# A gated recurrent cell and a tanh-shrink dense layer: the activation as a short polynomial, with a test and a second pass behind it

## The chip, the cores and the metric

One core of a Trainium2 chip. The metric is the device time of one execution of the whole kernel, in microseconds; lower is better.

## What is computed

The first half is an mLSTM cell over 4 x 8 heads, 768 steps and 40 features per head; the kernel computes it in chunks of 128 steps. Its output, rearranged to 3072 tokens of 320 features, goes through a dense pair of products with an activation between them:

```
def _moe_ref(x, w_in, w_out):
    h = x @ w_in            # 3072 x 320 by 320 x 2048
    g = h - np.tanh(h)
    return (g @ w_out).astype(np.float32)   # 2048 x 320
```

`w_in` and `w_out` arrive as 64-bit floats and are turned into 32-bit floats on the chip. All products are 32-bit.

## The kernel before

**The cell.** A unit is one chunk of one batch entry: 6 chunks x 4 entries make 24 units `n`. `cell_slot` (before L433) writes one slot of the cell: it fetches the inputs of the next unit (`fetch`), makes the decay matrix `E` of unit `s` by a scan on VectorE (`decay`, L348), takes its scores on TensorE (`score`, with the multiply by `E` on VectorE in L380), and for an older unit `o` the output (`inter`, `intra`), its normalisation (`gate`, L402 to L407) and the new state (`update`: product `pc`, then two adds on VectorE in L420). For a third unit `x` it transposes the result (`turn`, `px`, L89) and copies it into `xT` on ScalarE (L431). `ph`, `pc` and `px` share the two buffers of one PSUM pool, so `px` can only be written when the adds in L420 have emptied `pc`.

**The weights.** `convert` takes each 64-bit block apart: `w_e` and `w_m` on VectorE (L280, L283), then three ScalarE instructions (L281, L284, L285), then two on GpSimd (`w_r`, L286 and L287), then the sign on VectorE (L291), which writes `w_in` or `w_out`. There are 40 such blocks.

**The dense part.** Two units make a group `g` of 256 tokens, 12 groups; the 2048 hidden columns are 8 pairs `p` of 256. An item is one group by one pair, 96 in all. For an item `up` makes `h` in PSUM (`ph_up`, 6 products, each recorded as two instructions), `shrink` makes `g` in `gt`, and two items later (`LAG`) `down` adds 4 products into `po` (also two instructions each). `shrink` in the kernel before is four ScalarE instructions (L488 to L491: square, tanh, the square of a shifted square, and a mask) and five VectorE instructions (L492 to L496): a polynomial in `gt`, `h - tanh(h)` in `t`, and a copy of `t` into `gt` where `h` squared is over 0.1225:

```
A.activation(out=t, in_=ph, func=AF.Tanh)
A.activation(out=big, in_=z, func=AF.Relu, bias=border)
V.tensor_tensor(out=t, in0=ph, in1=t, op=OP.subtract)
V.copy_predicated(gt, big.bitcast(I32), t)
```

**The order.** Groups 0 to 5 are done in three passes over parts of the pairs (`PASSES`: pairs 0 and 1, 2 to 4, 5 to 7), since the weights of the later pairs are not converted yet. The first pass (12 items) is written between the cell's slots, about one item to a slot; the second pass (18 items) between the conversions of the last blocks; the remaining cell slots are spread over the later items. TensorE's order is fixed by hand (class `T` chains each of its instructions to the last). The other engines' orders come from the scheduler, and each engine runs its own in order. Loads are issued on SyncE's queue, the stores of the output on ScalarE's. All DMAs of both queues take eight completion semaphores in turn, and a DMA waits for the one that had its semaphore before.

Of the kernel before, what the change touches and what calls it, by code (L numbers as in the profile page):

```python
# [28 lines left out]
FP = mybir.dt.float32  # L32
BF = mybir.dt.bfloat16
I32 = mybir.dt.int32
I64 = mybir.dt.int64
U32 = mybir.dt.uint32
AF = mybir.ActivationFunctionType
OP = mybir.AluOpType
PSUM = bass.MemoryType.PSUM
NO_SYNC = mybir.DependencyInfo(mybir.DependencyClass.NoSync, mybir.DependencyReason.DATA)  # L40

L = 128


POLY = (-0.019838061344260048, -2.6070109206805303, -0.05287600604508702, 6.442407825412434)
# [9 lines left out]
def kernel(  # L55
# [13 lines left out]
    nc = tc.nc  # L69
    V, A, G = nc.vector, nc.scalar, nc.gpsimd  # L70
# [20 lines left out]
    B, NT, D, H, _ = qT.shape  # L91
    D1 = D + 1
    BH, S = i_gate.shape
    DM, DFF = moe_w_in.shape
    NFF = DFF // 128
    KC = [(c, min(128, DM - c)) for c in range(0, DM, 128)]
    NK = len(KC)
    NU = B * NT
    GT = 2
    TG = GT * L  # L100
    NG = NU // GT
    NP = NFF // 2
    HH = H // 2
    LAG = 2
    FIRST = 6
    NX = FIRST + 1
    PASSES = ((0, 1), (2, 4), (5, NP - 1))

    const = ctx.enter_context(tc.tile_pool(name="const", bufs=1))
    load = ctx.enter_context(tc.tile_pool(name="load", bufs=2))  # L110
    dram = ctx.enter_context(tc.tile_pool(name="dram", bufs=1, space=bass.MemoryType.DRAM))
    att = ctx.enter_context(tc.tile_pool(name="att", bufs=2))
    conv = ctx.enter_context(tc.tile_pool(name="conv", bufs=2))
    mlp = ctx.enter_context(tc.tile_pool(name="mlp", bufs=2))
    ps_h = ctx.enter_context(tc.tile_pool(name="ps_h", bufs=2, space=PSUM))
    ps_o = ctx.enter_context(tc.tile_pool(name="ps_o", bufs=1, space=PSUM))
    ps_a = ctx.enter_context(tc.tile_pool(name="ps_a", bufs=2, space=PSUM))
# [12 lines left out]
    TOP = SEC + D  # L130
    kz = [const.tile([128, H, L], FP, name=f"kz{i}") for i in range(2)]
    q2 = [const.tile([128, HH, L], FP, name=f"q2{i}") for i in range(2)]
    kp = [const.tile([L, HH, TOP], FP, name=f"kp{i}") for i in range(4)]
    v1 = [const.tile([L, H, D1], FP, name=f"v1{i}") for i in range(3)]
    for i in range(4):
# [9 lines left out]
    def load_unit(n):  # L145
# [7 lines left out]
        for r0, h0 in ((0, 0), (SEC, HH)):  # L153
            nc.sync.dma_start(out=t["kp"][:, :, r0:r0 + D], in_=k[b, c, :, h0:h0 + HH])
        t["o"] = load.tile([L, H, D], FP, name="o", tag="o", bufs=4)
        nc.sync.dma_start(out=t["o"], in_=o_gate[b, c])
# [6 lines left out]
    ones = const.tile([128, TOP], FP, name="ones")  # L163
    diag = const.tile([128, H, L], BF, name="diag")
    rebias = const.tile([128, 1], FP, name="rebias")
    square = const.tile([128, 1], FP, name="square")
    border = const.tile([128, 1], FP, name="border")
    V.memset(rebias, -896.0 * (1 << 23))
    V.memset(square, POLY[2])
    V.memset(border, -SMALL)  # L170
    make_identity(nc, ident)
    V.memset(ones, 1.0)
# [30 lines left out]
    for w in (after, ones):  # L203
        p = ps_b.tile([w.shape[1], NT, BH], FP, name="psum_lf", tag="b")
        T.matmul(p.rearrange("p c n -> p (c n)"), w, lfT.rearrange("p c n -> p (c n)"),
                 start=True, stop=True)
# [10 lines left out]
    xr, n, f = (mlp.tile([L, 2, NR], FP, name=name, tag=tag) for name, tag in (("xr", "z"), ("n", "z"), ("f", "q")))  # L217
# [34 lines left out]
    w_in = const.tile([128, NK, DFF], FP, name="w_in")  # L252
    w_out = const.tile([128, NFF, DM], FP, name="w_out")
# [63 lines left out]
    xT = [const.tile([128, NK, TG], FP, name=f"xT{i}") for i in range(NX)]  # L317
# [5 lines left out]
    for t in xT + qg + ys + sum(state, []):  # L323
        G.memset(t, 0.0)


    un = {}

# [95 lines left out]
    def turn(n, j):  # L424
        t = un[n]
        if j == 0:
            t["px"] = ps_b.tile([128, NK, L], FP, name="px", tag="b")
        T.transpose(t["px"][:, j, :], t["y"][:, j * 128:(j + 1) * 128], ident)
        if j == NK - 1:
            g, tt = divmod(n, GT)  # L430
            A.copy(out=xT[g % NX][:, :, tt * L:(tt + 1) * L], in_=t["px"])  # L431
            un.pop(n)

    def cell_slot(s, o, x):


        steps = []

        def begin():
            if o is not None:  # L440
                prepare(o)
            if s is not None and s - 1 in un:
                prepare(s - 1)
            if s is not None:
                if s + 1 < NU:
                    fetch(s + 1)
                decay(s)

        steps.append((0.0, begin))
        for d in range(HH):  # L450
            for i in range(2):
                if s is not None:
                    steps.append((0.22, lambda h=2 * d + i: score(s, h)))
                if o is not None and i == 0:
                    steps.append((0.22 if o >= B else 0.0, lambda d=d: inter(o, d)))
            if o is not None:
                steps += [(0.22, lambda h=h: intra(o, h)) for h in (d, d + HH)]
                if d in (1, 2) and o + B < NU:
                    steps += [(0.18, lambda j=j: update(o, j)) for j in (2 * d - 2, 2 * d - 1)]
        if o is not None:  # L460
            steps.append((0.0, lambda: gate(o)))
        if x is not None:
            steps += [(0.11, lambda j=j: turn(x, j)) for j in range(NK)]
        return steps


    gT, po = {}, {}
    lead, root, _, rest = POLY

    def up(g, p):  # L470
        ph = {}

        def product(i, j):
            if not ph:
                ph[0] = ps_h.tile([128, 2, TG], FP, name="ph_up", tag="ph")
            f = 2 * p + i
            T.matmul(ph[0][:, i, :], w_in[:, j, f * 128:(f + 1) * 128], xT[g % NX][:, j, :],
                     start=(j == 0), stop=(j == NK - 1))
            if (i, j) == (1, NK - 1):
                shrink(ph[0])  # L480

        def shrink(ph):
            z = mlp.tile([128, 2, TG], FP, name="z", tag="z")
            q = mlp.tile([128, 2, TG], FP, name="q", tag="q")
            t = mlp.tile([128, 2, TG], FP, name="t", tag="t")
            big = mlp.tile([128, 2, TG], FP, name="big", tag="big")
            gt = gT[g, p] = mlp.tile([128, 2, TG], FP, name="gt", tag="gt", bufs=LAG + 2)
            A.activation(out=z, in_=ph, func=AF.Square)  # L488
            A.activation(out=t, in_=ph, func=AF.Tanh)  # L489
            A.activation(out=q, in_=z, func=AF.Square, bias=square)  # L490
            A.activation(out=big, in_=z, func=AF.Relu, bias=border)  # L491
            V.scalar_tensor_tensor(out=gt, in0=ph, scalar=lead, in1=z, op0=OP.mult, op1=OP.mult)  # L492
            V.tensor_tensor(out=t, in0=ph, in1=t, op=OP.subtract)  # L493
            V.scalar_tensor_tensor(out=gt, in0=z, scalar=root, in1=gt, op0=OP.add, op1=OP.mult)  # L494
            V.scalar_tensor_tensor(out=gt, in0=q, scalar=rest, in1=gt, op0=OP.add, op1=OP.mult)  # L495
            V.copy_predicated(gt, big.bitcast(I32), t)  # L496

        return [(0.43, lambda i=i, j=j: product(i, j)) for i in range(2) for j in range(NK)]

# [96 lines left out]
        merge(dense, work[x])  # L596


# [39 lines left out]
```

## Time and profile before

| | |
|---|---|
| runs, median of 3 | 707.3 us (707.11 to 708.67) |
| profiled execution | 708.27 us, of it the span of instructions 706.6 us |
| TensorE matmuls | busy 625.3 us (89%) |
| VectorE | busy 541.0 us (77%) |
| ScalarE | busy 303.4 us (43%) |
| GpSimd | busy 164.5 us (23%) |
| TensorE's mean granted clock | 0.934 of full speed |
| DMA | 50.93 MB |

The shares are means over a span with two halves. Up to about 300 us the cell, the conversions and 21 items share the engines; after that 75 items and the rest of the cell run. So the table by stretches is what is to be read, then what each engine waits for in a stretch.

### The profile page before, as it was taken

What the parts mean: (1) busy time and instruction counts of PE and PEld (TensorE: products, weight loads), DVE (VectorE), ACT (ScalarE), POOL (GpSimd) and SP (SyncE); (2) the same over time, 40 slices, a digit from 0 to 9 for tenths busy, and PEclk for the clock granted to TensorE, in tenths of its full rate; (3) what the DMA queues carried; (4) which work ended last, traced back from release to release, by engine and by line L of the source; (5) the groups of instructions that cost most, each with busy time, mean ns of one, the idle gap of its engine ahead of it and who ended that gap; (6) DMA issues with size and microseconds to landing.
All of it is one profiled execution on the core that took longest, in us unless ns stands there. A gap on an engine that the chain in (4) does not pass through costs nothing.

```text
span 706.6 us, 9050 instructions
## 1 busy us (share of the span) xinstructions
PE 625.3 (89%) x3098; PEld 520.4 (74%) x3098; DVE 541.0 (77%) x897; ACT 303.4 (43%) x584; POOL 164.5 (23%) x190
## 2 busy tenths in 40 slices
PE   1277797797888985999999999999999999999997
PEld 1276696685777863678888888888888888878875
DVE  8677778887888798987768797776866766767764
ACT  3323143343532476654444343444534435454553
POOL 7535544445443267400002011010110000000000
PEclk9757689998988997999999999999999999999999
DMA  5657345554464443100003132220200000000000
GB/s 141 161 150 205 103 118 139 150 158 108 125 170 115 141 126 78 37 1 2 0 24 100 30 95 57 71 72 6 91 10 0 20 1 19 1 20 0 10 10 20
DMA packets 73278, 50.93 MB, mean 72 GB/s; under 512 B 53520, under 2 KB 60048, under 8 KB 73232
## 3 DMA queue, kind: packets, MB, share of 16 engines
q1 hardware_dynamic: 69360, 46.22, 23.8%
q10 hardware_dynamic: 3872, 4.13, 1.7%
q8 instruction: 25, 0.41, 0.2%
q14 instruction: 21, 0.17, 0.1%
HBM read 46.20 MB, written 4.13 MB: 71 GB/s over the span
## 4 chain that ended last, share of the span: by engine, by line
PE 69%; DVE 16%; POOL 5%; ACT 4%; issue 4%; DMA 2%; SPq 1%; ACTq 0%; POOLq 0%; DVEq 0%
PE ph_up L85 31%; PE po L85 25%; PE ps L85 5%; PE ph L85 5%; DVE E L348 3%; POOL w_r L286 2%; POOL w_r L287 2%; PE pc L85 1%; DVE gt L495 1%; DVE gt L494 1%; DVE gt L492 1%; DVE t L493 1%; DVE w_in L291 1%; PE px L89 1%; DVE E L380 1%
## 5 line engine op out<-in xcount | busy, mean ns | idle before, releaser
L85 PE MATMUL ph_up<-xT,w_in 128*128 128x256 f32 x1152 | 307.8, 394 | 2.3 <-DVE t L493 1.6
L85 PE MATMUL po<-w_out,gt 128*128 128x320 f32 x768 | 249.1, 449 | 10.7 <-DVE part L514 9.8
L85 PEld LDWEIGHTS ph_up<-xT,w_in 128*128 128x128 f32 x1152 | 209.7, 196 | 36.7 <-issue 3.9
L85 PEld LDWEIGHTS po<-w_out,gt 128*128 128x128 f32 x768 | 138.8, 195 | 49.7 <-DVE part L514 12.1
L488 ACT ACTIVATE z<-ph_up 128x512 f32<-128x512 f32 x96 | 57.2, 596 | 269.1 <-PE ph_up L85 263.5
L492 DVE SCALAR_TENSOR_TENSOR gt<-ph_up,z 128x512 f32<-128x512 f32 x96 | 66.0, 687 | 90.8 <-ACT t L489 90.7
L85 PE MATMUL ps<-q,kz 128*128 128x128 f32 x384 | 85.0, 323 | 17.5 <-DVE E L380 11.7
L85 PEld LDWEIGHTS ps<-q,kz 128*128 128x128 f32 x384 | 74.3, 228 | 25.8 <-DVE E L380 11.9
L496 DVE COPY_PREDICATED gt<-big,t 128x512 f32<-128x512 int32 x96 | 76.5, 796 | 6.5 <-DVE gt L495 0.5
L85 PEld LDWEIGHTS ph<-vw,E 128*128 128x128 f32 x384 | 69.4, 214 | 7.9
L495 DVE SCALAR_TENSOR_TENSOR gt<-q,gt 128x512 f32<-128x512 f32 x96 | 70.1, 730 | 6.5 <-DVE gt L494 0.5
L490 ACT ACTIVATE q<-z,square 128x512 f32<-128x512 f32 x96 | 69.4, 723 | 0.0
L491 ACT ACTIVATE big<-z,border 128x512 f32<-128x512 f32 x96 | 69.1, 720 | 0.0
L494 DVE SCALAR_TENSOR_TENSOR gt<-z,gt 128x512 f32<-128x512 f32 x96 | 67.5, 703 | 0.0
L493 DVE TENSOR_TENSOR t<-ph_up,t 128x512 f32<-128x512 f32 x96 | 65.3, 680 | 0.0
L85 PE MATMUL ph<-vw,E 128*128 128x41 f32 x384 | 61.9, 267 | 0.0
L489 ACT ACTIVATE t<-ph_up 128x512 f32<-128x512 f32 x96 | 56.8, 592 | 0.0
L348 DVE TENSOR_TENSOR_SCAN E<-E,diag 128x1024 f32<-128x1024 f32 x24 | 55.8, 2324 | 0.8 <-DMA E<-f_rows 0.8
L363 POOL TENSOR_TENSOR qg<-qg,q 104x512 f32<-104x512 f32 x20 | 28.2, 1410 | 117.4 <-DMA qg<-g_rows 90.1
L286 POOL TENSOR_TENSOR w_r<-w_r,w_m 128x256 f32<-128x256 f32 (+2 forms) x40 | 36.3, 907 | 56.2 <-ACT w_m L284 43.1
L366 POOL TENSOR_TENSOR vs<-v,eiS 128x328 f32<-128x328 f32 x20 | 17.7, 884 | 108.8 <-PE pc L85 108.8
L89 PE MATMUL px<-ident,ys 128*128 128x128 f32 x72 | 17.0, 305 | 26.5 <-DVE state L420 23.5
(87 smaller groups left out, 489.4 us busy)
## 6 DMA issues: line engine op xcount, KB each, us to landing
E<-f_rows SPq DMA_DIRECT2D x24, 512.0 KB
w<-in_moe_w_out SPq DMA_DIRECT2D x16, 320.0 KB
w<-in_moe_w_in SPq DMA_DIRECT2D x16, 256.0 KB
kz<-in_kT SPq DMA_DIRECT2D x48, 80.0 KB
q<-in_qT SPq DMA_DIRECT2D x48, 80.0 KB
v<-in_v SPq DMA_DIRECT2D x24, 160.0 KB
kp<-in_k SPq DMA_DIRECT2D x48, 80.0 KB
o<-in_o_gate SPq DMA_DIRECT2D x24, 160.0 KB
```

The lines of the kernel that those rows point to most:

```text
L85: return cls.keep(nc.tensor.matmul(*args, **kwargs))
L286: G.tensor_tensor(out=rf, in0=rf, in1=mf, op=OP.add)
L348: V.tensor_tensor_scan(out=row, data0=row, data1=diag.rearrange("p h t -> p (h t)"), initial=0.0, op0=OP.mult, op1=OP.add)
L488: A.activation(out=z, in_=ph, func=AF.Square)
L489: A.activation(out=t, in_=ph, func=AF.Tanh)
L490: A.activation(out=q, in_=z, func=AF.Square, bias=square)
L491: A.activation(out=big, in_=z, func=AF.Relu, bias=border)
L492: V.scalar_tensor_tensor(out=gt, in0=ph, scalar=lead, in1=z, op0=OP.mult, op1=OP.mult)
L493: V.tensor_tensor(out=t, in0=ph, in1=t, op=OP.subtract)
L494: V.scalar_tensor_tensor(out=gt, in0=z, scalar=root, in1=gt, op0=OP.add, op1=OP.mult)
L495: V.scalar_tensor_tensor(out=gt, in0=q, scalar=rest, in1=gt, op0=OP.add, op1=OP.mult)
L496: V.copy_predicated(gt, big.bitcast(I32), t)
```

## The change

`shrink` keeps two ScalarE and two VectorE instructions; the mask, the tanh and what used them are gone. The polynomial has other coefficients and holds for small `h` only. The first ScalarE instruction also writes, per partition, the sum of the 512 squares into one column of `sums`. Each group's `xT` is stored to device memory, on ScalarE's queue. At the end the largest sum of each partition is compared with 0.0224, the partitions over it are counted by one product, all five engines load the count into a register and branch. Where it isn't zero, the whole dense part is done again from the stored `xT` by the old nine instructions, and the output is overwritten.

```
 L = 128
+TINY_POLY = (0.05323766086013854, -1.252188626488792, 4.693255265604215)
+TINY = 0.0224
...
+    tiny = const.tile([128, 1], FP, name="tiny")
+    V.memset(tiny, TINY_POLY[1])
...
+    x_rows = dram.tile([NG, 128, NK, TG], FP, name="x_rows")
...
             A.copy(out=xT[g % NX][:, :, tt * L:(tt + 1) * L], in_=t["px"])
             un.pop(n)
+            if tt == GT - 1:
+                nc.scalar.dma_start(out=x_rows[g], in_=xT[g % NX])
...
+    sums = const.tile([128, NG * NP], FP, name="sums")
...
-            A.activation(out=z, in_=ph, func=AF.Square)
-            A.activation(out=t, in_=ph, func=AF.Tanh)
-            A.activation(out=q, in_=z, func=AF.Square, bias=square)
-            A.activation(out=big, in_=z, func=AF.Relu, bias=border)
-            V.scalar_tensor_tensor(out=gt, in0=ph, scalar=lead, in1=z, op0=OP.mult, op1=OP.mult)
-            V.tensor_tensor(out=t, in0=ph, in1=t, op=OP.subtract)
-            V.scalar_tensor_tensor(out=gt, in0=z, scalar=root, in1=gt, op0=OP.add, op1=OP.mult)
-            V.scalar_tensor_tensor(out=gt, in0=q, scalar=rest, in1=gt, op0=OP.add, op1=OP.mult)
-            V.copy_predicated(gt, big.bitcast(I32), t)
+            A.activation(out=z, in_=ph, func=AF.Square, accum_out=sums[:, g * NP + p:g * NP + p + 1])
+            A.activation(out=q, in_=z, func=AF.Square, bias=tiny)
+            V.scalar_tensor_tensor(out=gt, in0=ph, scalar=TINY_POLY[0], in1=z, op0=OP.mult, op1=OP.mult)
+            V.scalar_tensor_tensor(out=gt, in0=q, scalar=TINY_POLY[2], in1=gt, op0=OP.add, op1=OP.mult)
...
+    most = att.tile([128, 1], FP, name="most", tag="most")
+    V.tensor_reduce(out=most, in_=sums, axis=mybir.AxisListType.X, op=OP.max)
+    V.tensor_single_scalar(most, most, TINY, op=OP.is_gt)
+    count = ps_a.tile([1, 1], FP, name="count", tag="a")
+    T.matmul(count, most, ones[:, 0:1], start=True, stop=True)
+    again = att.tile([1, 1], I32, name="again", tag="again")
+    V.tensor_copy(out=again, in_=count)
...
+    with tc.If(nc.values_load(again, min_val=0, max_val=128,
+                              skip_runtime_bounds_check_because="it counts partitions") > 0):
+        for c in range(NT):
+            for bb in range(B // GT):
+                x = xT[bb]
+                nc.sync.dma_start(out=x, in_=x_rows[c * (B // GT) + bb])
...
+                    gt = shrink_any(ph)
...
```

**VectorE, one slot of the first pass.** `E<-E,diag` is the scan, `state` the adds that empty `pc`, `gt` and `t` the item's activation, `den` the normalisation of the older unit. Before:

```order
L348 SCALAR_TENSOR_TENSOR E<-E,diag 128x1024
L420 TENSOR_TENSOR state_1_235<-state_1_235,pc 40x4x41
L380 TENSOR_TENSOR E<-ps,E 128x512
L492 SCALAR_TENSOR_TENSOR gt<-ph_up,z 128x512
L493 TENSOR_TENSOR t<-ph_up,t 128x512
L494 SCALAR_TENSOR_TENSOR gt<-z,gt 128x512
L420 TENSOR_TENSOR state_1_235<-state_1_235,pc 40x4x41
L495 SCALAR_TENSOR_TENSOR gt<-q,gt 128x512
L380 TENSOR_TENSOR E<-ps,E 128x512
L496 COPY_PREDICATED gt<-big,t 128x512
L402 TENSOR_SCALAR den<-ph 128x8
L280 TENSOR_SCALAR w_e<-w_1229 128x320
```

The same slot with the change:

```order
L358 SCALAR_TENSOR_TENSOR E<-E,diag 128x1024
L430 TENSOR_TENSOR state_1_237<-state_1_237,pc 40x4x41
L390 TENSOR_TENSOR E<-ps,E 128x512
L500 SCALAR_TENSOR_TENSOR gt<-ph_up,z 128x512
L430 TENSOR_TENSOR state_1_237<-state_1_237,pc 40x4x41
L501 SCALAR_TENSOR_TENSOR gt<-q,gt 128x512
L390 TENSOR_TENSOR E<-ps,E 128x512
L412 TENSOR_SCALAR den<-ph 128x8
L288 TENSOR_SCALAR w_e<-w_1195 128x320
```

Two instructions are gone from ahead of the second `state` add, and a third from ahead of `den` and `w_e`; the rest stands as it did.

**ScalarE, the same slot.** `w_r`, `w_e` and `w_m` are the conversion, `part` a partial sum of the dense part, `xT` the copy behind the transposes. Before:

```order
L490 ACTIVATE q<-z,square 128x512
L491 ACTIVATE big<-z,border 128x512
L285 ACTIVATE w_r<-w_893 128x320
L285 ACTIVATE w_r<-w_907 128x256
L516 COPY part_215<-po 128x320
L431 COPY xT_210<-px 128x3x128
L516 COPY part_216<-po 128x320
L281 ACTIVATE w_e<-w_e,rebias 128x320
L284 ACTIVATE w_m<-w_m 128x320
```

With the change:

```order
L499 ACTIVATE q<-z,tiny 128x512
L293 ACTIVATE w_r<-w_878 128x320
L293 ACTIVATE w_r<-w_892 128x256
L521 COPY part_217<-po 128x320
L441 COPY xT_212<-px 128x3x128
L444 DMA x_rows<-xT_212 128x768
L289 ACTIVATE w_e<-w_e,rebias 128x320
L292 ACTIVATE w_m<-w_m 128x320
L521 COPY part_218<-po 128x320
```

In every second slot the store of `xT` now stands between the copy and the conversion's next block. Seven of the twelve stores are in the part of the order that the cell's first 17 slots fill.

**ScalarE, the end of the program.** `ob` is the last group's output. Before:

```order
L490 ACTIVATE q<-z,square 128x512
L491 ACTIVATE big<-z,border 128x512
L522 COPY ob<-po 128x320
L525 DMA out<-ob 128x320
L522 COPY ob<-po 128x320
L525 DMA out<-ob 128x320
L634 UNCONDITIONAL_BRANCH
```

With the change:

```order
L527 COPY ob<-po 128x320
L530 DMA out<-ob 128x320
L527 COPY ob<-po 128x320
L530 DMA out<-ob 128x320
L630 TENSOR_LOAD again
L630 COMPARE_AND_BRANCH
L619 ACTIVATE z<-ph_up 128x512
```

The register load and the branch follow the last store on this engine, and stand at the same place on the other four; what comes behind the branch is the second pass, which the branch passes over.

## Rows read from the trace of the kernel before

**Rows 1.** Windows: span; PE, PEld, DVE, ACT, POOL busy; PEclk, DMA share, GB/s.

```profile
50.00:100.00 50.00, 39.77 (x224) 37.27 (x225) 38.32 (x67) 14.89 (x35) 26.17 (x28) 0.73 0.55 153
100.00:250.00 150.00, 126.42 (x740) 108.88 (x740) 124.85 (x209) 58.04 (x125) 65.93 (x72) 0.90 0.48 131
250.00:300.00 50.00, 38.38 (x145) 28.35 (x144) 47.45 (x81) 32.68 (x71) 30.86 (x29) 0.90 0.31 85
300.00:706.60 406.60, 402.21 (x1903) 328.31 (x1901) 293.99 (x473) 183.31 (x327) 14.61 (x15) 1.00 0.10 29
```

**Rows 2.** The chain that ended last, late stretch: start, us, what.

```profile
688.34 2.59 PE ph_up L85 x12
690.93 2.15 PE po L85 x8
```

**Rows 3.** Waits of 100 to 250 us: who waited for whom, total, times, longest.

```profile
PE px L89 <- DVE state L420: 23.5, 7, 5.3
```

**Rows 4.** The scan on VectorE, first and last of eleven, from the timeline.

```profile
105.41 2.27 DVE L348 TENSOR_TENSOR_SCAN E<-E,diag 128x1024 f32<-128x1024 f32 x1
...
242.16 2.28 DVE L348 TENSOR_TENSOR_SCAN E<-E,diag 128x1024 f32<-128x1024 f32 x1
```

**Rows 5.** Timeline of one slot, VectorE's and ScalarE's waits in the conversion.

```profile
170.98 0.56 ACT L281 ACTIVATE w_e<-w_e,rebias 128x320 int32<-128x320 int32 x1 [1.44 <-DVE den L403]
174.39 1.00 DVE L291 SCALAR_TENSOR_TENSOR w_out<-w,w_r 128x320 int32<-128x320 int32 x1 [1.93 <-POOL w_r L287]
176.01 1.48 DVE L291 SCALAR_TENSOR_TENSOR w_in<-w,w_r 128x256 int32<-128x256 int32 x1 [0.62 <-POOL w_r L287]
```

**Rows 6.** Waits of 250 to 300 us.

```profile
PE po L85 <- DVE part L514: 9.6, 3, 7.9
```

**Rows 7.** Groups by line, whole span: busy us, mean ns | idle before, releaser.

```profile
L489 ACT ACTIVATE t<-ph_up 128x512 f32<-128x512 f32 x96 | 56.8, 592 | 0.0
L491 ACT ACTIVATE big<-z,border 128x512 f32<-128x512 f32 x96 | 69.1, 720 | 0.0
L492 DVE SCALAR_TENSOR_TENSOR gt<-ph_up,z 128x512 f32<-128x512 f32 x96 | 66.0, 687 | 90.8 <-ACT t L489 90.7
L493 DVE TENSOR_TENSOR t<-ph_up,t 128x512 f32<-128x512 f32 x96 | 65.3, 680 | 0.0
L494 DVE SCALAR_TENSOR_TENSOR gt<-z,gt 128x512 f32<-128x512 f32 x96 | 67.5, 703 | 0.0
L496 DVE COPY_PREDICATED gt<-big,t 128x512 f32<-128x512 int32 x96 | 76.5, 796 | 6.5 <-DVE gt L495 0.5
```

**Rows 8.** Windows of L493 alone: VectorE busy, PEclk, DMA share, GB/s.

```profile
100.00:250.00 150.00, 8.12 (x12) 0.90 0.48 131
250.00:300.00 50.00, 5.43 (x8) 0.90 0.31 85
```

**Rows 9.** The same of L494 alone.

```profile
100.00:250.00 150.00, 8.74 (x12) 0.90 0.48 131
250.00:300.00 50.00, 6.86 (x8) 0.90 0.31 85
```

**Rows 10.** The same of L496 alone.

```profile
100.00:250.00 150.00, 10.38 (x12) 0.90 0.48 131
250.00:300.00 50.00, 6.81 (x7) 0.90 0.31 85
```

**Rows 11.** Waits, whole span: ScalarE held by a store of the output.

```profile
ACT z L488 <- DMA out<-ob: 5.5, 2, 3.7
```

**Rows 12.** The end: timeline, then the instructions of the last line (ns, first to last).

```profile
700.40 2.42 PE L85 MATMUL po<-w_out,gt 128*128 128x320 f32 x8 [0.42 <-DVE gt L496]
703.67 0.34 ACTq L525 DMA_DIRECT2D out<-ob  x1
L634 SPq EVENT_SEMAPHORE  x7: 17/28/28, 705.5 to 706.5; - x7
```

**Rows 13.** Groups by line: the shortest kind of VectorE operation.

```profile
L402 DVE TENSOR_SCALAR den<-ph 128x8 f32<-128x8 f32 x24 | 3.8, 157 | 4.1 <-PE ph L85 4.1
```

More of the change, by code (lines that the diff above doesn't have):

```diff
@@ L467 @@
     gT, po = {}, {}
-    lead, root, _, rest = POLY
+    sums = const.tile([128, NG * NP], FP, name="sums")
     def up(g, p):
@@ L484, in shrink @@
             q = mlp.tile([128, 2, TG], FP, name="q", tag="q")
-            t = mlp.tile([128, 2, TG], FP, name="t", tag="t")
-            big = mlp.tile([128, 2, TG], FP, name="big", tag="big")
             gt = gT[g, p] = mlp.tile([128, 2, TG], FP, name="gt", tag="gt", bufs=LAG + 2)
-            A.activation(out=z, in_=ph, func=AF.Square)
-            A.activation(out=t, in_=ph, func=AF.Tanh)
-            A.activation(out=q, in_=z, func=AF.Square, bias=square)
-            A.activation(out=big, in_=z, func=AF.Relu, bias=border)
-            V.scalar_tensor_tensor(out=gt, in0=ph, scalar=lead, in1=z, op0=OP.mult, op1=OP.mult)
-            V.tensor_tensor(out=t, in0=ph, in1=t, op=OP.subtract)
-            V.scalar_tensor_tensor(out=gt, in0=z, scalar=root, in1=gt, op0=OP.add, op1=OP.mult)
-            V.scalar_tensor_tensor(out=gt, in0=q, scalar=rest, in1=gt, op0=OP.add, op1=OP.mult)
-            V.copy_predicated(gt, big.bitcast(I32), t)
+            A.activation(out=z, in_=ph, func=AF.Square, accum_out=sums[:, g * NP + p:g * NP + p + 1])
+            A.activation(out=q, in_=z, func=AF.Square, bias=tiny)
+            V.scalar_tensor_tensor(out=gt, in0=ph, scalar=TINY_POLY[0], in1=z, op0=OP.mult, op1=OP.mult)
+            V.scalar_tensor_tensor(out=gt, in0=q, scalar=TINY_POLY[2], in1=gt, op0=OP.add, op1=OP.mult)
         return [(0.43, lambda i=i, j=j: product(i, j)) for i in range(2) for j in range(NK)]
@@ L596, with shrink_any @@
         merge(dense, work[x])
+    most = att.tile([128, 1], FP, name="most", tag="most")
[5 more added lines that the diff above has]
+    V.tensor_copy(out=again, in_=count)
+    lead, root, _, rest = POLY
+    def shrink_any(ph):
+        z = mlp.tile([128, 2, TG], FP, name="z", tag="z")
+        q = mlp.tile([128, 2, TG], FP, name="q", tag="q")
+        t = mlp.tile([128, 2, TG], FP, name="t", tag="t")
+        big = mlp.tile([128, 2, TG], FP, name="big", tag="big")
+        gt = mlp.tile([128, 2, TG], FP, name="gt", tag="gt", bufs=LAG + 2)
+        A.activation(out=z, in_=ph, func=AF.Square)
+        A.activation(out=t, in_=ph, func=AF.Tanh)
+        A.activation(out=q, in_=z, func=AF.Square, bias=square)
+        A.activation(out=big, in_=z, func=AF.Relu, bias=border)
+        V.scalar_tensor_tensor(out=gt, in0=ph, scalar=lead, in1=z, op0=OP.mult, op1=OP.mult)
+        V.tensor_tensor(out=t, in0=ph, in1=t, op=OP.subtract)
+        V.scalar_tensor_tensor(out=gt, in0=z, scalar=root, in1=gt, op0=OP.add, op1=OP.mult)
+        V.scalar_tensor_tensor(out=gt, in0=q, scalar=rest, in1=gt, op0=OP.add, op1=OP.mult)
+        V.copy_predicated(gt, big.bitcast(I32), t)
+        return gt
@@ new lines @@
+    with tc.If(nc.values_load(again, min_val=0, max_val=128,
[4 more added lines that the diff above has]
+                nc.sync.dma_start(out=x, in_=x_rows[c * (B // GT) + bb])
+                ob = [ps_o.tile([128, DM], FP, name="po", tag=f"po{tt}") for tt in range(GT)]
+                for p in range(NP):
+                    ph = ps_h.tile([128, 2, TG], FP, name="ph_up", tag="ph")
+                    for i in range(2):
+                        f = 2 * p + i
+                        for j in range(NK):
+                            nc.tensor.matmul(ph[:, i, :], w_in[:, j, f * 128:(f + 1) * 128], x[:, j, :],
+                                             start=(j == 0), stop=(j == NK - 1))
+                    gt = shrink_any(ph)
+                    for i in range(2):
+                        for tt in range(GT):
+                            nc.tensor.matmul(ob[tt], gt[:, i, tt * L:(tt + 1) * L], w_out[:, 2 * p + i, :],
+                                             start=(p == 0 and i == 0), stop=(p == NP - 1 and i == 1))
+                for tt in range(GT):
+                    o = mlp.tile([128, DM], FP, name="ob", tag="ob")
+                    A.copy(out=o, in_=ob[tt])
+                    nc.scalar.dma_start(out=out[((bb * GT + tt) * NT + c) * L:((bb * GT + tt) * NT + c + 1) * L, :], in_=o)
```

## The prediction

> **What bounds the kernel now.** I read the table by stretches first. From 300 us to the end TensorE is busy 402.2 of 406.6 us at a granted clock of 1.00 [rows 1]. There the chain of work is products alone: 2.59 us for an item's 6 products into `ph_up`, 2.15 us for its 4 into `po` [rows 2], 4.74 us an item, and no instruction of the activation between them. That stretch is bound by TensorE, its products stay as they are, and nothing that VectorE or ScalarE is spared there can shorten it.
>
> Before 300 us it is otherwise. From 100 to 250 us VectorE is busy 124.9 of 150 us, TensorE 126.4, at a clock of 0.90. TensorE's idle time is 23.6 us [rows 1], and the waits of that stretch put 23.5 us of it, seven times, on one thing: the transpose `px` waits for the adds in L420, which empty the buffer that `px` is written to [rows 3]. VectorE does those adds in its queue behind the scan, the scores' multiply and the item's activation; the order in the section on the change shows `t` and the second `gt` just ahead of the second add. So here the activation lies on the path. A cell slot takes (242.16 - 105.41) / 10 = 13.7 us [rows 4]. VectorE has its own wait in each slot, 1.93 and 0.62 us in the one shown, for GpSimd's part of the weights' conversion [rows 5].
>
> From 250 to 300 us VectorE is busy 47.45 of 50 us and TensorE 38.4 [rows 1]; TensorE waits 9.6 us for an add into `part` that VectorE is late with [rows 6]. VectorE is the bound there.
>
> **The change, part by part.**
>
> *Three VectorE instructions less per item.* They are 0.680, 0.703 and 0.796 us in the mean, 2.18 us an item [rows 7]. In the three stretches:
>
> - 50 to 100 us: one item, 2.2 us. The rest of that stretch is start-up and conversion. I take 1.
> - 100 to 250 us: 8.12 + 8.74 + 10.38 = 27.2 us for 12 items [rows 8 to 10]. Ends: 0, if what VectorE no longer does turns into waiting for the conversion; 27.2, if all of it comes off. At its present clock TensorE can give back its 23.6 us of idle time and no more. I take 20: nearer to the upper end, because the wait that stops TensorE ends on an instruction that stands behind those removed, and short of 23.6 because VectorE's wait for GpSimd [rows 5] grows when VectorE comes to it sooner.
> - 250 to 300 us: 5.43 + 6.86 + 6.81 = 19.1 us [rows 8 to 10], but the 8 items there cost TensorE 8 x 4.74 = 37.9 us, so at most 12.1 of the 50 us can go. TensorE becomes the bound. Ends 5 (half the 9.6 us of rows 6) and 12; I take 10.
> - after 300 us: 75 items' worth is removed under TensorE's own work. Nothing; the cover is 402 us of products.
>
> Together 1 + 20 + 10 = 31 us.
>
> *Two ScalarE instructions less, and the sum in the first.* Tanh and mask were 0.59 and 0.72 us an item [rows 7]. ScalarE was busy 58 of 150 us in the middle stretch [rows 1], so this is worth something only as latency: the first `gt` waited for `t` on the same engine [rows 7], which is late no more. I count it as nothing. No row shows an instruction that writes a sum as well. Its cost lies between 0 and that of another instruction of this size, 0.6 us; either way ScalarE does less than before, so also nothing. `tiny` is one memset at the start.
>
> *The stores of `xT`.* Seven lie in the part before 300 us. Each is 128 x 768 x 4 = 384 KB. A DMA issue holds ScalarE 0.34 us [rows 12]. At 131 GB/s the engines were 0.48 busy [rows 1], so a store takes some 393 / 273 = 1.4 us of all of them, in a stretch where half their time is free. On ScalarE the store stands ahead of the conversion's `w_e`, where ScalarE waited 1.44 us in the slot shown [rows 5]; that covers the issue. What it need not cover is a wait for the semaphore that an earlier load still holds: two of the 24 output stores held ScalarE 5.5 us together, 3.7 the longer [rows 11]. Ends 0 and 7 x 3.7 = 26 us; I take 2, nearest to the mean of rows 11 (0.23 us) for seven.
>
> *The test at the end.* The reduction needs the last sum only and runs beside the last products. After the last product, at 702.8 us, the order is: one product of a single column (2.42 / 8 = 0.30 us), the cast (near L402's 0.16 us [rows 13]), the register load, the compare, the jump, and the join. The last store, issued at 703.7 us, is waited for until about 705.5 us [rows 12], so 2.7 us are covered. The trace shows neither a load of a register from memory nor a taken branch. Below, I bound each by nothing; above, by a round trip to memory, which that store shows as 705.5 - 703.7 = 1.8 us. There are three at most: the load, the jump over the second pass, the jump at its end. So the end gets between 0 and 0.46 + 3 x 1.8 - 2.7 = 3.2 us longer. I take 3, since the second pass stands between branch and target on every engine that has a part in it.
>
> The Trainium skill speaks against the change here. "Runtime: NRT & Kernel Launch", section "Instruction fetch mechanics", says that instructions are prefetched in sequence only, and that a taken branch to a target outside the present pages waits for the fetch of the target's page. No row of this kernel shows that. By the page, the upper end of 3.2 us would be the one to take; without it, the cost of a branch would be the issue of an instruction, and the end would stay covered.
>
> *Sum.* 31 - 2 - 3 = 26 us off. The profiled execution took 708.3 us, 1.0 above the median of the runs: 682.3 by its time, **681** at the median's level.
>
> **The rivals.**
>
> 1. *The front is held by something else.* With VectorE shorter, the conversion's path through ScalarE and GpSimd, or the loads, hold the slot. For it: VectorE's waits on GpSimd are there in every slot [rows 5], and the DMA engines are half busy. Against: TensorE's waits name the adds [rows 3]. Then of TensorE's 23.5 us some 8 come back, 5 in the third stretch, less 5 for stores and test: 699 us.
>
> 2. *The stores take it back, and it is slower.* Place: ScalarE's queue in every second slot. Each store waits for the load that has its semaphore, and SyncE's next load on that semaphore waits for the store. At 3.7 us [rows 11] and a landing of 1.8 us [rows 12], all of it on the path, seven stores cost 38 us against 28 (31 less 3): 717 us. It decides above 28 / 7 = 4.0 us a store. Against it: such waits came up in 2 of 24 output stores, though with the DMA engines 0.10 busy [rows 1].
>
> 3. *The second pass runs.* The change then doesn't do what it says. The largest sum that the reference's own inputs give is 0.0123, under 0.0224; but the sums are 512 squares of about 0.0031 squared, 0.005 a column, and if ScalarE's accumulator ran on from one instruction to the next, the fifth column would be over. Then 96 x 4.74 = 455 us of products come on top, about 1137 us.
>
> 4. *All of VectorE's work comes off*: 2.2 + 27.2 + 19.1 - 5 = 43.5 us, with TensorE's clock raised because it idles less: 664 us.
>
> **How the numbers follow.** Forecast 0.67 (664 to 695), rival 1 0.20, rival 2 0.09, rival 3 0.02, rival 4 0.02. A difference of under 0.2% (1.4 us) is about what a measurement of this kernel cannot tell from none. Of rival 1, 0.03 lies within that, of rival 2 0.01. Faster: 0.67 + 0.17 + 0.02 = 0.86; same 0.04; slower 0.08 + 0.02 = 0.10. The range goes from 664, where everything removed counts, to 700, which takes in most of rival 1; it leaves out rivals 2 to 4 and a quarter of rival 1, 0.18 in all.
>
> **What would show it.** Right: TensorE's waits for L420's successor (L430) between 100 and 250 us fall from 23.5 us to some 5; a slot takes about 12 us in place of 13.7; 21 items are done by about 272 us; from there on 4.74 us an item at a clock of 1.00, as before. The stores hold ScalarE under 0.5 us each, and the span ends some 7 us after the last product in place of 3.8. Wrong: VectorE's share in the front falls and the slot stays at 13.7 us, its idle time then ending on GpSimd or a DMA (rival 1); ScalarE waits for microseconds at the stores (rival 2); products after the test (rival 3); or the test takes more than the 3.2 us.

## The result, and the profile of the changed kernel

The changed kernel takes 687.6 us in the median of four runs (685.9 to 690.7), the kernel before took 708.0 beside it (707.1 to 710.0): a ratio of 0.9713 [0.9669, 0.9757]. The runs of this kernel lie some 3 us to either side of their median, so a difference between two variants below that is not read as one. Forecast were 681, in a range of 664 to 700.

The profiled execution's span is 687.0 us against 706.6, which is 19.6 us less. Where they came off is read first from the table by stretches (span; busy time of PE, PEld, DVE, ACT and POOL; granted clock, DMA share, GB/s), which answers to [rows 1]:

```profile
50.00:100.00 50.00, 38.80 (x223) 36.54 (x223) 35.03 (x64) 12.80 (x32) 24.06 (x27) 0.73 0.56 157
100.00:250.00 150.00, 132.69 (x799) 112.87 (x798) 109.02 (x197) 59.88 (x143) 90.96 (x89) 0.97 0.58 162
250.00:300.00 50.00, 43.25 (x176) 33.62 (x175) 29.53 (x47) 21.57 (x49) 16.95 (x15) 0.93 0.15 43
300.00:687.00 387.00, 381.10 (x1819) 311.45 (x1817) 141.41 (x236) 110.04 (x237) 14.24 (x15) 1.00 0.12 35
```

VectorE went from 124.9 to 109.0 us of the middle stretch and from 47.5 to 29.5 of the third. In both it now has less work than TensorE; what TensorE still waits for is read below. TensorE's clock in the middle rose from 0.90 to 0.97, and it had 17.3 us of idle time there in place of 23.6. The scan is the mark of a cell slot. These are the 8th and the 18th in the timeline of VectorE (start, us), the counterparts of [rows 4]:

```profile
105.16 2.28 DVE L358 TENSOR_TENSOR_SCAN E<-E,diag 128x1024 f32<-128x1024 f32 x1
...
226.52 3.20 DVE L358 TENSOR_TENSOR_SCAN E<-E,diag 128x1024 f32<-128x1024 f32 x1
```

The 19.6 us therefore split so. The 8th scan starts 0.25 us earlier (105.41 to 105.16). The ten slots take 121.4 us in place of 136.8, 15.4 less: 12.1 us a slot for 13.7. From the 18th scan to the end it is 460.5 in place of 464.4, 3.9 less. The last number holds an end that is 2.2 us longer, so some 6 us came off ahead of it.

These are times of one execution each. The run with a short second pass, below, has the same order of instructions up to the branch; there the 8th scan comes at 103.55 us and ten slots take 117.6, so the split is good to 2 to 4 us.

The ten slots by themselves, before and with the change (columns as above):

```profile
105.41:242.16 136.75, 113.17 (x666) 97.51 (x666) 112.33 (x190) 49.83 (x108) 59.94 (x66) 0.89 0.52 142
105.16:226.52 121.36, 106.42 (x675) 91.80 (x674) 87.45 (x161) 42.50 (x100) 70.27 (x66) 0.96 0.61 169
```

TensorE's idle time fell from 23.6 to 14.9 us, which is 8.6 of the 15.4. The other 6.8 are its products: no fewer of them, 675 recorded for 666, took 106.4 us in place of 113.2, at a granted clock of 0.96 in place of 0.89 (1.00 is 2.4 GHz throughout, less is a mix with 1.2 GHz).

What is late now in the middle stretch? The waits of 100 to 250 us (who waited for whom, total, times, longest), beside [rows 3]:

```profile
PE px L95 <- DVE state L430: 13.7, 8, 2.7
POOL qg L373 <- DMA qg<-g_rows: 12.7, 6, 3.4
DVE w_in L299 <- POOL w_r L295: 12.3, 10, 2.1
ACT o L381 <- DMA o<-in_o_gate: 11.7, 5, 3.2
DVE E L358 <- DMA E<-f_rows: 9.8, 5, 2.7
DVE w_out L299 <- POOL w_r L295: 8.3, 6, 1.9
```

TensorE's wait for the adds fell from 23.5 us to 13.7, not to 5. Three of the six rows end on loads: `qg`, `o` and `E`. The kernel before waited 0.3 us for `qg` in this stretch and 0.8 for `E` in its whole span. What holds the loads stands in SyncE's queue, 50 to 250 us:

```profile
SPq L157 <- POOL qg L373: 63.8, 12, 9.1
SPq L156 <- DMA x_rows<-xT: 7.4, 2, 4.4
SPq L276 <- DMA x_rows<-xT: 6.6, 2, 5.6
SPq L162 <- DMA x_rows<-xT: 5.7, 1, 5.7
SPq L257 <- DMA x_rows<-xT: 5.2, 1, 5.2
```

Six loads waited, 24.9 us together, for a store of `xT` that had their completion semaphore before them. On ScalarE the same stores are cheap: each issue held that queue 0.33 us in the median, 0.39 at most.

In the third stretch TensorE still waits for an add into `part` (timeline: start, us, instruction, idle time before it and what ended it), as in [rows 6]:

```profile
258.53 3.86 PE L91 MATMUL po<-w_out,gt 128*128 128x320 f32 x8 [6.75 <-DVE part L519]
```

VectorE's timeline around it tells why:

```profile
250.26 0.68 DVE L501 SCALAR_TENSOR_TENSOR gt<-q,gt 128x512 f32<-128x512 f32 x1
250.86 1.18 DVE L291 TENSOR_SCALAR w_m<-w 128x320 int32<-128x320 int32 x2
252.81 1.00 DVE L288 TENSOR_SCALAR w_e<-w 128x256 int32<-128x256 int32 x1 [0.76 <-POOL w_r L295]
...
257.07 0.41 DVE L299 SCALAR_TENSOR_TENSOR w_in<-w,w_r 128x256 int32<-128x256 int32 x1
257.40 0.67 DVE L500 SCALAR_TENSOR_TENSOR gt<-ph_up,z 128x512 f32<-128x512 f32 x1
258.00 0.47 DVE L519 TENSOR_TENSOR part<-po,part 128x320 f32<-128x320 f32 x1
```

The add stands behind a run of the last blocks' conversion that fills VectorE's queue from 250.9 to 257.4 us. The engine isn't full in this stretch (29.5 of 50 us); the order is what holds the add.

After 300 us TensorE is busy without a gap up to the last item, and the chain that ended last repeats an item each 4.74 us as before:

```profile
667.19 2.59 PE ph_up L91 x12
671.93 2.59 PE ph_up L91 x12
674.52 5.94 PE po L91 x22
```

The groups by line (busy us, mean ns | idle before, releaser) show the sum as an instruction of its own, L498, and GpSimd's `qg` slower, 2090 ns in the mean against 1410 before:

```profile
L498 ACT ACTIVATION_READ_ACCUMULATOR z<-ph_up 128x1 f32 x96 | 18.6, 194 | 0.0
L500 DVE SCALAR_TENSOR_TENSOR gt<-ph_up,z 128x512 f32<-128x512 f32 x96 | 66.0, 688 | 202.5 <-ACT z L498 202.3
L373 POOL TENSOR_TENSOR qg<-qg,q 104x512 f32<-104x512 f32 x20 | 41.8, 2090 | 128.0 <-DMA qg<-g_rows 98.7 <-DMA q<-in_qT 28.2 <-issue 1.2
```

Last, the end, which answers to [rows 12]: the timeline, and then the instructions of the branch (ns, first to last start).

```profile
674.36 6.62 PE L91 MATMUL po<-w_out,gt 128*128 128x320 f32 x24
680.91 0.19 PE L91 MATMUL count<-ones,most 128*1 128x1 f32 x2
681.83 0.34 ACTq L530 DMA_DIRECT2D out<-ob  x1
```

```profile
L630 DVEq TENSOR_LOAD <-again x1: 695/695/695, 681.3 to 681.3; - x1
L630 SPq COMPARE_BRANCH  x1: 50/50/50, 681.9 to 681.9; - x1
L630 PEldq COMPARE_BRANCH  x1: 3762/3762/3762, 681.9 to 681.9; - x1
L630 DVEq COMPARE_BRANCH  x1: 72/72/72, 682.1 to 682.1; - x1
L630 DVEq EVENT_SEMAPHORE  x1: 21/21/21, 685.5 to 685.5; - x1
L630 ACTq EVENT_SEMAPHORE  x1: 17/17/17, 686.0 to 686.0; - x1
```

The last output product ends at 674.36 + 6.62 = 681.0 us and the span 6.0 us later; before it was 3.8. The register loads take 0.48 to 0.70 us. The way past the second pass takes 3.8 us on TensorE and, from the compare to the next instruction, 3.3 on VectorE and 3.1 on ScalarE (compare at 682.8). SyncE's compare takes 0.05.

### The profile page after: what moved, and what is told of

Its sections match the earlier page's. It is cut to its first block, busy times and chain, and to the rows that moved or that the text cites. A ratio compares the mean times of both kernels' runs of the same rounds, so it can differ in the third digit from the quotient of the medians.

```text
span 687.0 us, 8555 instructions
## 1 busy us (share of the span) xinstructions
PE 614.5 (89%) x3100; PEld 512.2 (75%) x3100; DVE 351.4 (51%) x613; ACT 218.8 (32%) x488; POOL 174.0 (25%) x190
## 4 chain that ended last, share of the span: by engine, by line
PE 70%; DVE 13%; DMA 6%; POOL 4%; issue 3%; ACT 3%; SPq 1%; ACTq 0%; POOLq 0%; DVEq 0%
PE ph_up L91 32%; PE po L91 27%; PE ps L91 4%; PE ph L91 4%; DVE E L358 3%; DMA E<-f_rows 3%; POOL w_r L294 2%; POOL w_r L295 2%; DMA w<-in_moe_w_in 1%; DVE E L390 1%; PE px L95 1%; PE pc L91 1%; DMA qg<-g_rows 1%; DVE gt L500 1%; DVE w_e L288 1%
## 5 line engine op out<-in xcount | busy, mean ns | idle before, releaser
L91 PE MATMUL ph_up<-xT,w_in 128*128 128x256 f32 x1152 | 303.2, 389 | 2.9 <-DVE gt L500 2.1
L91 PE MATMUL po<-w_out,gt 128*128 128x320 f32 x768 | 244.7, 443 | 7.0 <-DVE part L519 6.8
L91 PEld LDWEIGHTS ph_up<-xT,w_in 128*128 128x128 f32 x1152 | 206.2, 192 | 36.1 <-DVE gt L500 2.6
L498 ACT ACTIVATE z<-ph_up 128x512 f32<-128x512 f32 x96 | 57.2, 596 | 313.9 <-PE ph_up L91 313.9
L373 POOL TENSOR_TENSOR qg<-qg,q 104x512 f32<-104x512 f32 x20 | 41.8, 2090 | 128.0 <-DMA qg<-g_rows 98.7
L499 ACT ACTIVATE q<-z,tiny 128x512 f32<-128x512 f32 x96 | 69.2, 721 | 2.8
L390 DVE TENSOR_TENSOR E<-ps,E 128x512 f32<-128x512 f32 x48 | 32.9, 686 | 20.0 <-PE ps L91 19.4
L295 POOL TENSOR_TENSOR w_r<-w_r,w_e 128x256 f32<-128x256 f32 (+2 forms) x40 | 34.5, 863 | 2.7
L91 PEld LDWEIGHTS ph<-state,qg 128*128 128x128 f32 x160 | 29.6, 199 | 5.8 <-issue 0.5
L95 PE MATMUL px<-ident,ys 128*128 128x128 f32 x72 | 16.5, 296 | 17.2 <-DVE state L430 13.7
L289 ACT ACTIVATE w_e<-w_e,rebias 128x256 int32<-128x256 int32 (+2 forms) x40 | 21.0, 526 | 28.0 <-DVE w_e L288 24.7
L91 PE MATMUL ph<-state,qg 128*128 128x82 f32 x160 | 28.9, 264 | 0.2 <-issue 0.2
```

Of the source, the lines that this page charges most:

```text
L91: return cls.keep(nc.tensor.matmul(*args, **kwargs))
L95: return cls.keep(nc.tensor.transpose(*args, **kwargs))
L289: A.activation(out=e, in_=e, func=AF.Relu, scale=8.0, bias=rebias[0:p])
L295: G.tensor_tensor(out=rf, in0=rf, in1=e.bitcast(FP), op=OP.mult)
L373: G.tensor_tensor(out=t["qg"][0:TOP], in0=t["qg"][0:TOP], in1=t["q2"][0:TOP], op=OP.mult)
L390: V.tensor_tensor(out=P, in0=t["ps"], in1=P, op=OP.mult)
```

## The experiments

The theory after this profile: the three VectorE instructions are the gain, the stores take back more than the 2 us forecast by holding SyncE's loads, and the end costs 2. The rivals: ScalarE's two instructions are part of the gain; the loads hold the front with the stores or without; the test's cost is larger than the end shows.

**Without the stores.** The second pass stays, without its loads.

```
-    x_rows = dram.tile([NG, 128, NK, TG], FP, name="x_rows")
-            if tt == GT - 1:
-                nc.scalar.dma_start(out=x_rows[g], in_=xT[g % NX])
-                nc.sync.dma_start(out=x, in_=x_rows[c * (B // GT) + bb])
```

> The changed kernel without the twelve stores of xT; the second pass, which does not run, is left without its loads. Theory: with VectorE shorter the loads are what is late in the cell's slots (VectorE waited 13.5 us for E in the changed kernel, 0.8 before), and the stores add to it through bytes and shared semaphores; so 3 to 7 us less than the changed kernel's 687.6, about 682 to 685, and VectorE's wait for E halved. Rival: the stores use DMA time that is free; within 1 us of 687.6, and the wait for E stays near 13 us.

Measured: 680.5 us, 0.96 [0.9564, 0.9637]. The interval does not touch that of the changed kernel, and the medians lie 7.1 us apart. Ten slots take 114.0 us, 22.8 less than before. Two of its waits between 100 and 250 us:

```profile
PE px L95 <- DVE state L429: 6.7, 6, 1.5
DVE E L357 <- DMA E<-f_rows: 8.8, 8, 2.0
```

TensorE's wait for the adds is down to nearly what was forecast for the changed kernel. Its idle time in the ten slots is 9.3 us, at a clock of 1.00:

```profile
103.85:217.84 113.99, 104.71 (x686) 89.43 (x686) 87.79 (x161) 44.00 (x102) 72.55 (x67) 1.00 0.59 161
```

The wait for `E` did not shrink by half: the loads are late in a slot of 11.4 us without any store too. So the edit brings some 7 us, more than was expected, but not by way of `E`. It does a little more than it says: without the stores the scheduler also orders the conversion otherwise (see the held stores).

**Without the test and the second pass.** Everything from `most` on is cut; stores and sums stay.

```
-    most = att.tile([128, 1], FP, name="most", tag="most")
...
-    with tc.If(nc.values_load(again, min_val=0, max_val=128,
...
```

> The changed kernel without the reduction, the count, the branch and the second pass; the stores and the sums stay. Theory: the test costs what the trace of the changed kernel shows behind the last product, 5.9 us in place of 3.8, so 2 us less than 687.6, about 685.5, all of it behind the last product. Rival: the second pass costs more by the length of the program, or less since the end is hidden: outside 1 to 3 us.

Measured: 684.1 us, 0.9669 [0.9635, 0.9703]. That is 3.6 us under the changed kernel, with intervals that overlap; the 2.2 us read at the end fit. This run alone doesn't set the size. Ten slots take 118.0 us here, with the changed kernel's stores and order, for its 121.4.

**The activation alone.** Stores, test and sums are cut, the short polynomial stays.

```
-            A.activation(out=z, in_=ph, func=AF.Square, accum_out=sums[:, g * NP + p:g * NP + p + 1])
+            A.activation(out=z, in_=ph, func=AF.Square)
```

> The short activation alone: no sums, no stores, no test, so the result holds for small h only. Theory: the gains of the two edits before add, 5 to 9 us less than 687.6, about 679 to 683. Rival: the sums' own instruction on ScalarE (0.19 us, 96 times) is on the path in the front: a further 3 us or more below what the two edits give together.

Measured: 680.5 us, 0.9615 [0.9584, 0.9647]. It is what the kernel without stores took, so the test's 2 us and the sums' instruction are not seen in this pair. Both intervals are some 5 us wide. What the sums cost, if anything, stays under what these runs tell. Against the run without the test, which has stores and sums, it is 3.6 us less, with intervals that overlap.

**ScalarE's two instructions back, unread.** To the kernel with the activation alone:

```
+            A.activation(out=t, in_=ph, func=AF.Tanh)
+            A.activation(out=big, in_=z, func=AF.Relu, bias=border)
```

> The short activation alone as in the run before, but ScalarE still computes tanh and the mask, which nothing reads. Theory: ScalarE's two instructions were worth next to nothing, VectorE's three are the gain; within 2 us of the run before. Rival: the shorter ScalarE queue (tanh and mask stood ahead of the conversion's instructions) is a good part of the gain: 4 us or more above the run before.

Measured: 676.8 us, 0.9581 [0.9542, 0.962]. That is 3.7 us under the run before, with intervals that overlap, where the theory had it within 2. Nothing is lost; ScalarE's part of the change is worth nothing that can be measured.

**VectorE's three instructions back, unread.** To the same kernel:

```
+            V.tensor_tensor(out=t, in0=ph, in1=z, op=OP.subtract)
+            V.scalar_tensor_tensor(out=t2, in0=z, scalar=1.0, in1=t, op0=OP.add, op1=OP.mult)
...
+            V.copy_predicated(t2, z.bitcast(I32), t)
```

> The short activation alone (no sums, stores or test), with three VectorE instructions per item added whose result nothing reads, of the shapes of the three that the change removed; ScalarE has its two. Theory: VectorE's queue is what bounds the front, so the gain of 27.5 us is given back: 702 to 709. Rival: what counted was where the removed instructions stood (two of them waited for tanh and the mask), or ScalarE; then at least 8 us of the gain stay, under 700.

Measured: 711.6 us, 1.0046 [1.0026, 1.0067]. The whole gain is gone, and the three take 0.68, 0.72 and 0.76 us each, near those of [rows 7]. Ten slots take 132.8 us, and from the 18th scan to the end it is 469.7. Its windows are near those of [rows 1] again:

```profile
100.00:250.00 150.00, 125.91 (x757) 107.58 (x756) 130.12 (x210) 48.86 (x105) 67.66 (x74) 0.93 0.48 131
250.00:300.00 50.00, 35.51 (x133) 25.77 (x132) 47.30 (x81) 24.95 (x55) 32.60 (x30) 0.91 0.30 83
```

```profile
PE px L95 <- DVE state L429: 23.3, 8, 4.3
```

The wait for the adds is back at 23.3 us, and VectorE's wait for `E` is gone: that load is late only when VectorE is fast. With the run before it this settles which engine the gain came from.

**Stores of one row.** Is it the bytes of the stores, or that there is a store? One partition of the 128 is written; the orders on SyncE and VectorE stay those of the changed kernel.

```
-                nc.scalar.dma_start(out=x_rows[g], in_=xT[g % NX])
+                nc.scalar.dma_start(out=x_rows[g][0:1], in_=xT[g % NX][0:1])
```

> The changed kernel, but each store of xT moves one partition of 128 (3 KB in place of 384); the second pass, which does not run, is left without its loads. The orders of SyncE and VectorE are those of the changed kernel. Theory: the stores cost through the semaphores that they share with the loads: SyncE holds a load until a store has been issued and has landed (24.9 us in the changed kernel's front). A small store still has to be issued and to land, so SyncE's waits for it stay above 12 us and the time within 3 us of the changed kernel's 687.6. Rival: it is the bytes; then the time falls to that of the run without stores, 680.5.

Measured: 686.1 us, 0.9673 [0.9636, 0.971]. SyncE still waited for stores twice before 250 us, 9.7 us together, less than expected:

```profile
SPq L257 <- DMA x_rows<-xT: 5.8, 1, 5.8
SPq L162 <- DMA x_rows<-xT: 3.9, 1, 3.9
```

The ten slots take 114.4 us, as without stores, which speaks for the bytes; but the 8th scan comes at 108.45 us, 4.6 later than without stores, and the total is the changed kernel's within the scatter. SyncE's waits for stores fell from 24.9 to 9.7 us and the time did not follow. Bytes, held semaphores and the order of the instructions, which is the changed kernel's on every engine, are not told apart by this.

**Five stores, late.** `xT` has seven buffers, so the last seven groups are still on the chip at the end. Only groups 0 to 4 are stored, each six groups later; the second pass takes the resident groups first.

```
-            if tt == GT - 1:
-                nc.scalar.dma_start(out=x_rows[g], in_=xT[g % NX])
+            if tt == GT - 1 and 0 <= g - 6 < NG - NX:
+                nc.scalar.dma_start(out=x_rows[g - 6], in_=xT[g - 6])
```

> All that the change does, with five stores in place of twelve: xT of groups 5 to 11 stays on the chip to the end, and groups 0 to 4 are stored when group 6 to 10 has been transposed, so that one store is at the end of the front and four behind 300 us, where TensorE bounds. Theory: the time of the run without stores, 680.5, within 2 us; SyncE does not wait for a store before 250 us. Rival: the wait for the store moves to a load of the late part and holds TensorE there: 684 or more.

Measured: 686.6 us, 0.9702 [0.9673, 0.9731], no gain. The edit didn't do what it says. The scheduler put the five stores where their data was ready, not where they were written:

```profile
L444 ACTq DMA_DIRECT2D x_rows<-xT x5: 327/344/348, 61.3 to 171.2; - x5
```

**Five stores, held late.** The same, with each store tied in the order behind the copy that it is written after.

```
+            done = A.copy(out=xT[g % NX][:, :, tt * L:(tt + 1) * L], in_=t["px"])
...
+                late = nc.scalar.dma_start(out=x_rows[g - 6], in_=xT[g - 6])
+                tc.add_manual_dep(late.ins, done.ins.name, NO_SYNC, reason="stores behind the front")
```

> The run with five late stores again, now with each store tied behind the copy of group 6 to 10 in ScalarE's order, since the scheduler had moved them ahead to 61 to 171 us. Theory: what the stores cost comes off with them; the time of the run without stores, 680.5, within 2 us, no wait of SyncE for a store before 200 us, and the last scan of the front at about 218 us in place of 226.5. Rival: the earlier run without stores was faster by the scheduler's order alone; 685 or more.

Measured: 682.1 us, 0.9622 [0.9585, 0.966]. The interval lies under that of the changed kernel, whose test and second pass it has in full: it is the best complete version here. Its stores, SyncE's only wait for one between 50 and 250 us, and TensorE's wait from 100 to 250 us:

```profile
L444 ACTq DMA_DIRECT2D x_rows<-xT x5: 333/333/351, 217.0 to 562.6; - x5
```

```profile
SPq L156 <- DMA x_rows<-xT: 1.1, 1, 1.1
```

```profile
PE px L95 <- DVE state L430: 7.0, 7, 1.6
```

Ten slots take 114.3 us. So 5.5 us come back when the stores stand behind the front. Its rival, the scheduler's order, is not ruled out by that. Up to 300 us this run and the one without stores have one and the same order on every engine, and it is not the changed kernel's: 21 places of ScalarE's order, 14 of GpSimd's and 2 of VectorE's differ, mostly steps of the conversion that changed places with copies of `part` and with the cell's work on GpSimd. No run has the changed kernel's order without its stores.

**`E` loaded ahead of the rest.** `E` is the last load of a unit. To the kernel with five late stores, and then to the one with held stores from unit 8 on only:

```
+        E = att.tile([L, H, L], FP, name="E", tag="E", bufs=4)
+        spread(E, f_rows, n, 0)
...
-        t["E"] = att.tile([L, H, L], FP, name="E", tag="E", bufs=4)
-        spread(t["E"], f_rows, n, 0)
```

> The run with five late stores, and the load of E issued ahead of the unit's other loads in place of behind them. Theory: without early stores VectorE still waits some 12 us for E; with E first in SyncE's queue that wait falls under 4 us and the time by 4 to 8 us, to 673 to 677. Rival: SyncE is held by the other loads' buffers (63.8 us for qg's), E is late for the queue and not for its place in it, or another load becomes late in its stead: within 2 us of the run with late stores.

Measured: 686.4 us, 0.9701 [0.9674, 0.9728]. VectorE's wait for `E` is 3.5 us where the run with five late stores has 12.1, and the time is the same; two loads of L156 now waited 15.1 us for a store.

> The same, with the load of E ahead of the unit's other loads from unit 8 on (the earlier run had it so from the start, which put the third scan off from 43 to 53 us). Theory: VectorE's wait for E falls from 12 us to under 4 and 3 to 7 us come off the run with held stores: 674 to 678. Rival: the wait moves to another load; within 2 us of the run with held stores.

Measured: 685.8 us, 0.969 [0.9656, 0.9724], against 682.1 without this edit. The wait for `E` is 4.0 us in place of 13.6, the 18th scan comes 5.9 us earlier (215.4 for 221.2), and from there to the end it takes 7.8 us longer (469.5 for 461.7). What `E` gained went elsewhere: between 50 and 250 us TensorE waits 13.4 us for `ys`, the output that VectorE normalises, in place of 4.0. The edit also reordered VectorE, so this is not the loads alone; loading `E` first brought nothing in either kernel.

**A short second pass.** One group of twelve behind the branch:

```
-        for c in range(NT):
-            for bb in range(B // GT):
+        for c in range(1):
+            for bb in range(1):
```

> The changed kernel, but the second pass has one group in place of twelve, so it would redo a twelfth only. Theory: what the end costs is the jump over the second pass (3.76 us on TensorE, 3.4 on VectorE, against 0.05 on SyncE, which has 14 loads to jump over): with a shorter pass the jump shrinks on VectorE and ScalarE, and the end behind the last product goes from 5.9 to under 4.8 us; 687.6 less 1 to 2. Rival: a jump costs the same whatever its length; the end stays at 5.9 us.

Measured: 685.0 us, 0.9689 [0.9654, 0.9724]. Rows of its branch, as above:

```profile
L630 PEldq COMPARE_BRANCH  x1: 4158/4158/4158, 677.6 to 677.6; - x1
L630 DVEq EVENT_SEMAPHORE  x1: 21/21/21, 678.1 to 678.1; - x1
L630 ACTq EVENT_SEMAPHORE  x1: 17/17/17, 678.7 to 678.7; - x1
```

VectorE and ScalarE are past the branch within 0.3 us of their compare (677.8 and 678.5), where they needed 3.3 and 3.1. TensorE, with one group's products still to pass over, needs 4.2, no less than over twelve groups (3.8 in the changed kernel, 4.2 in the run without stores), and the span ends 6.1 us after the last output product, where it was 6.0. So the theory held for two engines, and for the end, which TensorE sets, the rival did. The 2.6 us under the changed kernel's median are not read as a gain.

What a long jump waits for stands in the trace's packets. Behind the changed kernel's branch the queues that load instructions move a block of 16 KB, from 682.93 us for 1.43, and three of 8 KB between 683.20 and 684.15. With the short second pass it is the 16 KB block alone (678.64 us, for 1.78), and of the engines TensorE alone is held; without the test there is none behind 656 us.

**The second pass made to run.** The kernel with held stores and a limit that the sums exceed:

```
-TINY = 0.0224
+TINY = 0.001
```

> The run with held stores with 0.001 in place of 0.0224 for the largest sum, so that the second pass runs. Theory: 96 items at 4.74 us are 455 us, with some 15 us for the start and the first load: 1140 to 1165 us. Rival: the second pass is bound by VectorE or by its latency, since nothing there is two items ahead: 1300 or more.

Measured in one run: 1149.1 us. TensorE is busy 461 of the 467 us from 680 on:

```profile
680.00:1147.00 467.00, 461.35 (x1903) 352.98 (x1902) 305.48 (x480) 229.23 (x407) 0.00 (x0) 1.00 0.04 13
```

Where the test fails, the kernel takes 467 us more, 1.62 times the time before.

## Why the prediction was right, and where not

**The bound of the front: right.** VectorE's activation was on TensorE's path there. ScalarE's two instructions back cost nothing, VectorE's three cost everything.

**After 300 us, nothing: right.** TensorE was busy 370.0 of the 370 us from 300 to 670 at a clock of 1.00, and the item stayed at 4.74 us.

**50 to 100 us: 1 taken, 0.25 came**, and 1.6 without the stores; the scatter of single executions is larger than either.

**100 to 250 us: 20 taken.** Net of the stores 15.4 came in ten slots, without them 22.8; with the stores held late it was 22.4. The size stands, but in part by luck. The term was to come out of TensorE's idle time alone, "at its present clock". Of the 15.4 us, 8.6 are idle time, and 14.3 of the 22.8; the rest is products that ran at a higher clock, 0.89 before, 0.96 with the change and 1.00 without stores, which only the fourth rival reckoned with.

**The stores: 2 taken, 4 to 7 measured.** This is the term that failed. It took the mean of [rows 11], output stores in a stretch where the DMA engines were 0.10 busy, and asked only whether ScalarE would be held. ScalarE was not (0.33 us a store). Without the stores it is 7.1 us less, with the stores held late 5.5; between the two runs without a test, of which one has stores and sums, it is 3.6. At no more than some 1 us a store before 300 us, they never came near the 4 us at which rival 2 decided. The lower end of 0 and the upper of 26 held it. That adding them in this place costs this is shown; the way it does is not. SyncE's loads waited 24.9 us for them, as rival 2 had it in its second half, but with stores of one row that fell to 9.7 us and the total stayed (686.1). The traffic, and the order into which the scheduler put the other instructions, are open beside it.

**250 to 300 us: 10 taken, some 6 came**, and some 4 without the stores (464.4 - 462.8 from the 18th scan on, and 2.2 of the end), under the lower end of 5. The cause is read, not tried: the add that empties `po` still waits behind a run of conversions that the scheduler put together, and TensorE 6.75 us for it (6.7 without the stores). VectorE had the time, but not in that order. The 21st item's `gt` was done at 277.0 us (303.8 before), not 272.

**The test: 3 taken, 2.2 measured** (6.0 us after the last product for 3.8). The size was right by two errors that cancel: the register load was 0.5 to 0.7 us and not up to 1.8, and one jump took 3.8 us and not up to 1.8. The Trainium skill's rule ("Runtime: NRT & Kernel Launch", section "Instruction fetch mechanics"), that a taken branch to a target beyond the pages at hand waits for a fetch, agrees with these rows: 3.1 to 3.8 us over a long second pass, 0.05 on SyncE's compare and some 0.2 on the two engines of the short second pass. The 16 KB block that is loaded behind the branch, in both kernels, is that fetch.

**The rivals.** The first (the front held by something else, 699 us) is there in small: loads are the late thing now. It did not decide, since the slot went to 12.1 us and, without stores, 11.4. The third didn't come about; made to, it took 1149 us where 1137 was worked out from 455 us of products. The fourth, 664, was never near: the best variant without any guard is at 677. Its condition, a higher clock, did come.

## What to carry to other kernels

An engine that is 77% busy in the mean can be the bound of a quarter of the span: take the work off where the waits of that stretch name it, and test the claim by putting the work back unread. A store added for a rare second pass is not priced by its issue alone (0.33 us each here, for 4 to 7 us in all): look at the loads that wait for it and at what the scheduler reorders around it. The scheduler puts it where its data is ready unless it is tied; tied behind the stretch that loads, it gave most of its price back here. An edit that takes something out can change the order of the rest: compare the orders before a difference is put down to the edit. The test at the end cost 2.2 us, set by the engines whose next instructions had to be loaded.

## What the runs showed of the hardware that was not expected

- The sum that an activation writes beside its result is a separate ScalarE instruction of 0.194 us each time.
- A taken branch took 3.8 us on TensorE over the whole second pass and 4.2 over a twelfth of it, while VectorE went from 3.3 us to 0.2 with that cut. In both kernels a block of 16 KB of instructions was loaded during TensorE's jump.
- A register load from on-chip memory took 0.48 to 0.51 us on four engines and 0.695 on VectorE.
- In the ten slots TensorE's granted clock was 0.89, 0.96 and 1.00 (before, with the change, without stores) where its idle time was 23.6 of 136.8, 14.9 of 121.4 and 9.3 of 114.0 us.
